# Forming five quads of weight sums from the staged plain quads in the last phase, with a written split plan per step

## The chip, the cores and the metric

The kernel runs on one core of one Trainium2 chip. The metric is the device time of one launch in microseconds (us); lower is better. The times shown are medians over runs. A profile is of one execution, and it lists its own time beside its span (first to last instruction).

## The reference, cut to what matters

A parallel block on `x` of shape (2048, 640), all in float32:

```python
xn = _layernorm(x, axis=-1)
return x + _A_ref(xn, A_wqkv, A_wo) + _B_ref(xn, B_w_gate, B_w_up, B_w_down)

# A: sliding-window attention, 32 heads of 20, window 256, then  o @ wo      (640 x 640)
# B: h = gelu(xn @ w_gate) * (xn @ w_up);  h @ w_down                        (1728 x 640)
```

The attention output `o` (640 features) and the first 1664 features of `h` are put one below the other, and `w_down` and `wo` too. So the last product is one product with 18 row blocks of 128, plus a rest of 64 features of `h`.

## The kernel before

Products are made in float32 from pairs of reduced-precision numbers. Every operand is **split** into a high part (ScalarE copies it into the type fp32r) and a low part (VectorE subtracts the high part from the original), and three matmuls (high by high, low by high, high by low) stand for one.

There are three phases. In the first, layer norm, projections and attention run, with a part of the gate and up products as filler. In the **gate phase** (about 652 to 838 us of the profile) the remaining gate and up products are made by `gate_up_pair`. In the **last phase** (from 837.8 us) the output product runs. Both phases after attention use a seven-product scheme for 2 x 2 blocks (Strassen's, in Winograd's form), which needs sums of blocks of both operands beside the plain blocks.

**Steps of the last phase.** The output is made in `NP` = 8 parts `p` of 256 rows. A part has ten steps: nine quads `k` = 0 to 8 (a quad is a 2 x 2 arrangement of four weight blocks of 128 x 320: two row blocks by two column halves), and one short step "e" for the rest of 64 features. Steps are numbered `n` = 0 to 79; "e" is the fifth of each ten (n = 4, 14, 24). Part 0 and the first four quads of part 1 are **plain** (24 matmuls per step, no sums needed). From n = 15 on (part 1, k = 4 to 8, and all later parts) a step takes 21 matmuls and needs, beside the plain quad `("b", k)`, the quad of sums `("t", k)`. From part 2 on the order of k is 4 to 8 and then 0 to 3.

**One pass of the step loop** (lines 1344 to 1372) puts into the queues: `load_step(n + 4)` on SP (activations of a later step), `split_step(n + 2)` (L1071: high part on ScalarE L1084, low part on VectorE L977), then `prepare(n)` (splits of weight quads for later), then the matmuls of step n (`terms`, L1142). At the last step of a part comes `drain`, which adds the PSUM banks of the finished part to the output rows on VectorE (L1165) and stores them from SP (L1168). The matmuls of the next part write the same banks, so the first of them waits for the first additions of the drain. The order on PE, ScalarE (ACT), VectorE (DVE) and SP is as written; each engine works off its queue in that order.

**Weight quads.** A quad is loaded into a staging tile `stg` (three buffers, L954) by `fetch`, and split by `high_quad` (ACT, L970) and `low_quad` (DVE, L974, which shows as its helper's line L977). In the last phase the fetches go out from ACT's own queue (`eng=nc.scalar`), so a fetch waits there for its staging buffer to come free, and what follows on ACT waits behind it. Quads b0 to b3 are split at the end of the gate phase; b4 to b8 and all t quads in the last phase. Two t quads have no room of their own: t7 is written over block 1 of b4 to b7, and t3 over block 1 of b0 to b3 (`borrow`), once the plain steps no longer need them.

**Where the sums are made before.** In the gate phase, `Job("t", q)` loads the plain quad into a tile `ats`, forms the four sums in place with four VectorE instructions (L977, L993, L977, L977), and stores the tile to `wtd[q]` in DRAM. Nine such jobs run among the others (`Job("o")` divides the attention output by its softmax sums, `Job("r")` makes the reciprocals). `work(cap)` is called between the products of `gate_up_pair` and does at most `cap` items. In the last phase all nine t quads are fetched from `wtd`.

**The plan before.** `tasks` gives one quad per step: the high part of b4 to b8 at n = 1 to 5, of t4, t5, t6, t7, t8, t0, t1, t2 at n = 6 to 13, and of t3 at n = 15. The low part follows one step later. The fetch of a quad goes out three places ahead, from ACT's queue, in n = 2 to 12.

Of the kernel before, what the change touches and what calls it, by code (L numbers as in the profile page):

```python
# [9 lines left out]
F32 = mybir.dt.float32  # L10
F32R = mybir.dt.float32r
BF = mybir.dt.bfloat16
AF = mybir.ActivationFunctionType
OP = mybir.AluOpType
# [20 lines left out]
HD = D // 2  # L35
HR = 5
NQD = 9
# [24 lines left out]
def block_kernel(ctx, tc, x, wqk, wv, wgu, wdo, wdl, out):  # L62
    nc = tc.nc

    const = ctx.enter_context(tc.tile_pool(name="const", bufs=1))
    dram = ctx.enter_context(tc.tile_pool(name="dram", bufs=1, space=DRAM))
# [16 lines left out]
    od = [dram.tile([D, C], F32, name=f"od{c}") for c in range(NC)]  # L83
    sd = [dram.tile([H, C], F32, name=f"sd{c}") for c in range(NC)]
    td = [{i: dram.tile([128, 2, C], F32, name=f"td{p}{i}") for i in (1, 2, 3, 4)} for p in range(NC // 2)]
    wtd = [dram.tile([128, 4, HD], F32, name=f"wtd{q}") for q in range(NQD)]
    rd = [dram.tile([H, C], F32, name=f"rd{c}") for c in range(NC)]
    hd = [dram.tile([NC, 128 if f < NF - 1 else 64, C], F32, name=f"hd{f}") for f in range(NF)]

# [836 lines left out]
    quads, staged, raws, ats = {}, {}, {}, {}  # L926
    place = {("b", 0): "xh1", ("b", 1): "xl1", ("b", 2): "xh0", ("b", 3): "xl0",
             ("t", 0): "xh2", ("t", 1): "xl2", ("t", 2): "xh3", ("t", 8): "xl3"}
    borrow = {7: 4, 3: 0}
# [10 lines left out]
    def four(t):  # L940
        return t.rearrange("p k (h n) -> p (k h) n", h=2)

    def fetch(kind, q, where="stg", eng=nc.sync):
        if where == "wr":
            ts = [wrp.tile([128, KT, 128], F32, name="wr", tag="wr").rearrange("p k m -> p (k m)") for _ in range(2)]
        elif where != "stg" and where != "at":
            ts = [tp.tile([128, D], F32, name=f"b{n}{q}", tag=f"x{n}{where}") for n in "hl"]
        if where != "stg" and where != "at":
            for i, t in enumerate(ts):
                nc.sync.dma_start(t, wdo[q][:, i])  # L950
            staged[kind, q] = [(t.rearrange("p (h n) -> p h n", h=2), slice(2 * i, 2 * i + 2)) for i, t in enumerate(ts)]
            return
        pool, bufs = (rp3, 3) if where == "stg" else (cp, 3)
        t = pool.tile([128, 4, HD], F32, name="stg", tag=where, bufs=bufs)  # L954
        eng.dma_start(t, four(wdo[q]) if kind == "b" else wtd[q])
        if kind == "t" and q in borrow:
            staged[kind, q] = [(t[:, i:i + 1], slice(i, i + 1)) for i in range(4)]
        else:
            staged[kind, q] = [(t, slice(0, 4))]

    def parts(kind, q):
        for raw, dst in staged[kind, q]:
            if kind == "t" and q in borrow:
                yield raw, quads["b", borrow[q] + dst.start], slice(1, 2)
            else:
                yield raw, slots(kind, q)[0][0], dst

    def high_quad(kind, q):
        for raw, t, dst in parts(kind, q):
            nc.scalar.activation(t[:, 0, dst], raw, AF.Copy)  # L970

    def low_quad(kind, q):
        for raw, t, dst in parts(kind, q):
            sub(t[:, 1, dst], raw, t[:, 0, dst].bitcast(F32))  # L974

    def sub(o, i, j, op=OP.subtract):
        nc.vector.tensor_tensor(out=o, in0=i, in1=j, op=op)  # L977

    class Job:
# [3 lines left out]
        def load(self):  # L983
            kind, i = self.kind, self.i
            if kind == "r":
                t = self.t = c2.tile([128, 128], F32, name="rc", tag="rc", bufs=2)
                nc.sync.dma_start(t, sd[i].rearrange("h (a t) -> (h a) t", a=4))
                self.items = [lambda: nc.vector.reciprocal(t, t)]
            elif kind == "t":
                t = self.t = cp.tile([128, 4, HD], F32, name="ats", tag="at", bufs=3)  # L990
                nc.sync.dma_start(t, four(wdo[i]))
                self.items = [lambda: sub(t[:, 0], t[:, 1], t[:, 0]), lambda: sub(t[:, 1], t[:, 3], t[:, 1], OP.add),
                              lambda: nc.vector.scalar_tensor_tensor(t[:, 3], t[:, 3], -1.0, t[:, 0],  # L993
                                                                     op0=OP.mult, op1=OP.subtract),
                              lambda: sub(t[:, 2], t[:, 2], t[:, 3], OP.add)]
            else:
                n = len(self.ks)
                if self.ks[0] == 0:
                    rbs[i] = c2.tile([128, C], F32, name="rb", tag="rb")
                    for k in range(4):  # L1000
                        nc.sync.dma_start(rbs[i][32 * k:32 * k + 32], rd[i])
                rows = self.rows = od[i][self.ks[0] * 128:(self.ks[-1] + 1) * 128].rearrange("(k p) t -> p k t", p=128)
                t = self.t = cp.tile([128, n, C], F32, name="ato", tag="at", bufs=3)
                nc.sync.dma_start(t, rows)
                self.items = [lambda k=k: sub(t[:, k], t[:, k], rbs[i], OP.mult) for k in range(n)]
# [8 lines left out]

    rbs = {}
    jobs = [Job("r", 0), Job("r", 1)]
    for c, qs_, r in ((0, (4, 5), 2), (1, (6, 7), 3), (2, (8, 0), None), (3, (1, 2), None)):
        jobs += [Job("t", q) for q in qs_] + [Job("o", c, (0, 1, 2)), Job("o", c, (3, 4))]
        jobs += [Job("r", r)] if r else []
    jobs.append(Job("t", 3))  # L1020
    going = []
    hook = [0]

# [219 lines left out]
    def split_later_xs(i, nxt=None):  # L1243
        def fn():
            split_xs(1, i, later[i])
            if nxt:
                later[nxt] = load_xs(1, nxt)
        return fn
# [9 lines left out]
    for j, f in enumerate(range(NFA, NF - 1)):  # L1258
        end = f + 1 == NF - 1
        first, second = {i: [] for i in range(4)}, {i: [] for i in range(4)}  # L1260
        first[0] += carry
        if j == 0:
            first[0].append(split_later_xs(2, 4))
            first[2].append(split_later_xs(1))
            first[3].append(split_later_xs(3))
            second[0].append(split_later_xs(4))
        if not end:
            nxt_w, sums = [], {}

            def next_tiles(j=j, raws=raws_next[f + 1]):  # L1270
                nxt_w.append(w_tiles(raws, *pools[(len(sets) + j + 1) % 2]))

            first[3].append(next_tiles)
            items = w_sums(raws_next[f + 1], sums)
            second[2] += items[0:2]
            second[3].append(items[2])
            carry = list(items[3:5])
            if f + 2 < NF - 1:
                second[3].append(load_next(f + 2))
        if j:  # L1280
            for i, n in enumerate((0, 3, 1, 2)):
                first[i].append(work(n))
        if not end:
            for i, n in enumerate((2, 3, 1, 1) if j else (0, 2, 1, 1)):
                second[i].append(work(n))
        else:
            fetch("b", 0, "wr")
            raw13 = cp.tile([128, D], F32, name="raw13", tag="r13")
            nc.sync.dma_start(raw13, wdl)
        gate_up_pair(f, w, 0, first)  # L1290
        if end:
            assert not jobs and not going
            for n in range(2):
                load_step(n)
            fetch("b", 1, "at")

            def quad(q):
                high_quad("b", q)
                low_quad("b", q)

            second[0].append(lambda: quad(0))
            second[0].append(lambda: [fetch("b", 2, "02"), fetch("b", 3, "03")])
            second[1].append(lambda: [split_step(0), load_step(2)])
            second[2].append(lambda: [split_step(1), quad(1), load_step(3)])
            second[3].append(lambda: [quad(2), split_step(2)])
        stores = gate_up_pair(f, w, 1, second, end)
        if end:
            quad(3)
        if not end:
            w = nxt_w[0], sums  # L1310
# [9 lines left out]
    psn = p3.enter_context(tc.tile_pool(name="psn", bufs=1, space=PSUM, reuse_waits="tile"))  # L1320
    w13 = rp3.tile([128, 2, D], F32R, name="w13")

    order_ = [("b", q) for q in range(4, NQD)] + [("t", q) for q in (4, 5, 6, 7, 8, 0, 1, 2)]
    tasks = {n + 1: q for n, q in enumerate(order_)}
    tasks[len(order_) + 2] = "t", 3
    turns = list(tasks)
    fetch_at = {0: [tasks[n] for n in turns[1:3]]}
    for i, n in enumerate(turns[3:]):
        fetch_at.setdefault(turns[i] + 1, []).append(tasks[n])

    def prepare(n):
        if n in tasks:
            high_quad(*tasks[n])
        if n - 1 in tasks:
            low_quad(*tasks[n - 1])
        if n == 2:
            nc.scalar.activation(w13[:, 0], raw13, AF.Copy)
            sub(w13[:, 1], raw13, w13[:, 0].bitcast(F32))
        for q in fetch_at.get(n, ()):
            fetch(*q, eng=nc.scalar if n else nc.sync)  # L1340

    fetch("b", 4)
    held = []
    for n, (p, k) in enumerate(steps):
        i = n % (NQD + 1)
# [71 lines left out]
```

## Time and profile before

| quantity | value |
|---|---|
| device time, median of 3 runs | 1090.1 us (1087.86 to 1091.1) |
| device time of the profiled execution | 1088.03 us |
| its span | 1086.3 us |
| busy: PE, DVE, ACT, POOL | 1068.9, 766.0, 511.9, 340.7 us |
| granted TensorE clock | 1.00 |
| DMA traffic | 162.31 MB, mean 149 GB/s |
| `ats<-wdo`, `wtd<-ats`, `stg<-wtd` transfers | 9 each, 640 KB |
| gate phase, matmuls L884 on the chain that ended last | 666.34 to 825.7 us, 702 matmuls |
| last phase, first and last matmul L1142 | 837.79 us, about 1083 us |

The chain that ended last, by engine: PE 84%, DVE 8%, DMA 4%. A matmul row with a count ("x96") is a run of instructions merged into one; its start and length are those of the run. A bracket at the end of a row gives the idle time of that engine just before it and what ended it. The ends of matmuls are modelled: a 128x320 matmul is listed with about 0.31 us, while in a run they start 0.147 us apart.

### The profile page before, as it was taken

To read this page: it belongs to the slowest core of one execution; us is meant where nothing else is said; L and a number is where in the kernel's file an instruction comes from. 1 tells how busy PE (TensorE), PEld (TensorE's weight loads), DVE (VectorE), ACT (ScalarE), POOL (GpSimd) and SP (SyncE) were. 2 spreads that over 40 slices of the span, in tenths; PEclk is the share of its full clock that TensorE was granted. 3 is DMA by queue.
4 is the path that set the end of the run, shared out by engine and by line. 5 is a ranking of instruction groups with operands and counts; after the bars stand their busy time and mean duration, and the time that the engine had idled before them with its cause. 6 is when DMAs were issued, how large, how long until landed. Compare 5 with 4: busy or idle time off the path is not lost.

```text
span 1086.3 us, 20868 instructions
## 1 busy us (share of the span) xinstructions
PE 1068.9 (98%) x7253; PEld 856.2 (79%) x7253; DVE 766.0 (71%) x2030; ACT 511.9 (47%) x1037; POOL 340.7 (31%) x513
## 2 busy tenths in 40 slices
PE   8999999999999999999999999999999989999998
PEld 7887767666778766676766668888888988999998
DVE  7755667666666576666767636888875669888887
ACT  4434655565644555465545465322234544333332
POOL 5022755577653373645446250211110000000000
PEclk9999999999999999999999999999999999999999
DMA  5651453546442244434233215588856873343433
GB/s 205 198 151 50 119 153 98 154 116 183 138 141 82 71 141 127 131 94 126 87 117 109 80 59 195 185 271 291 266 203 235 303 244 113 118 131 120 132 125 115
DMA packets 96058, 162.31 MB, mean 149 GB/s; under 512 B 13248, under 2 KB 57920, under 8 KB 95952
## 3 DMA queue, kind: packets, MB, share of 16 engines
q1 hardware_dynamic: 93280, 153.50, 44.6%
q10 hardware_dynamic: 2672, 7.47, 2.1%
q8 instruction: 57, 0.93, 0.4%
q14 instruction: 49, 0.40, 0.1%
HBM read 104.40 MB, written 56.23 MB: 148 GB/s over the span
## 4 chain that ended last, share of the span: by engine, by line
PE 84%; DVE 8%; DMA 4%; issue 1%; ACT 1%; SPq 0%; POOL 0%; ACTq 0%; DVEq 0%
PE ps_d L101 25%; PE ps L1142 15%; PE ps_g L884 15%; PE ps_o L547 8%; PE ps_e L520 7%; PE ps_m L464 7%; PE ps_v L101 5%; DVE junk L466 2%; PE ps_g L101 1%; DMA stg<-wtd 1%; DMA stg<-wdo 1%; DMA xi<-x 1%; PE ps_t L177 1%; DMA out<-xr 1%; DVE xi L160 1%
## 5 line engine op out<-in xcount | busy, mean ns | idle before, releaser
L466 DVE CUSTOM_DVE_ANT_0 junk<-ps_m,mask 128x384 bf16<-128x384 f32 (+2 forms) x512 | 271.9, 531 | 177.8 <-PE ps_m L464 132.9
L522 ACT ACTIVATE P<-ps_e 128x512 f32<-128x512 f32 (+2 forms) x384 | 197.6, 568 | 59.7 <-PE ps_e L520 52.9
L1142 PE MATMUL ps<-wb,at 128*128 128x320 f32 x999 | 157.8, 310 | 4.8 <-ACT wb L970 2.2
L1142 PEld LDWEIGHTS ps<-wb,at 128*128 128x128 f32 x999 | 149.0, 188 | 6.9 <-ACT wb L970 2.4
L533 POOL TENSOR_SCALAR_AFFINE_SELECT P<-P 128x512 f32<-128x512 f32 x128 | 86.6, 676 | 159.1 <-ACT P L522 155.0
L101 PE MATMUL ps_d<-xh,wql 128*128 128x512 f32 x430 | 129.2, 410 | 0.0
L101 PE MATMUL ps_d<-xh,wqh 128*128 128x512 f32 x430 | 128.5, 409 | 0.1
L101 PE MATMUL ps_d<-xl,wqh 128*128 128x512 f32 x430 | 128.6, 408 | 0.0
L464 PE MATMUL ps_m<-ks,qs 120*128 120x128 bf16 (+1 forms) x704 | 120.1, 275 | 1.4 <-DVE mx L466 1.1
L520 PE MATMUL ps_e<-qs,ks 122*128 122x128 bf16 (+2 forms) x704 | 112.4, 277 | 0.2
L520 PEld LDWEIGHTS <-ks 122*128 122x128 bf16 x704 | 49.9, 98 | 52.9 <-issue 41.9
L101 PEld LDWEIGHTS ps_d<-xl,wqh 128*128 128x128 f32 x430 | 78.3, 188 | 15.3 <-issue 1.2
L1142 PE MATMUL ps<-wt,at 128*128 128x320 f32 x552 | 89.0, 309 | 0.8 <-DVE xr L1165 0.8
L101 PEld LDWEIGHTS ps_d<-xh,wqh 128*128 128x128 f32 x430 | 77.7, 188 | 15.0 <-issue 1.0
L101 PEld LDWEIGHTS ps_d<-xh,wql 128*128 128x128 f32 x430 | 77.9, 189 | 14.6 <-issue 1.0
L464 PEld LDWEIGHTS <-qs 120*128 120x128 bf16 x704 | 62.2, 98 | 29.2 <-issue 11.6
L547 PE MATMUL ps_o<-P,v 128*32 128x384 f32 (+2 forms) x1408 | 84.3, 386 | 0.0
L1142 PEld LDWEIGHTS ps<-wt,at 128*128 128x128 f32 x552 | 82.9, 188 | 1.2 <-DVE xr L1165 1.0
L536 POOL TENSOR_SCALAR_AFFINE_SELECT P<-P 128x512 f32<-128x512 f32 x112 | 73.7, 668 | 27.9 <-ACT P L522 27.8
L238 POOL TENSOR_TENSOR pt<-r,pt 128x512 bf16<-128x512 f32 x40 | 46.8, 1171 | 103.7 <-ACT pt L237 89.6
L1096 ACT ACTIVATE at<-ss 128x512 fp32r<-128x512 f32 x59 | 37.3, 631 | 79.9 <-DVE ss L977 79.8
L547 PEld LDWEIGHTS ps_o<-P,v 128*32 128x32 f32 x1408 | 40.1, 110 | 39.5 <-issue 28.6
(185 smaller groups left out, 1701.3 us busy)
## 6 DMA issues: line engine op xcount, KB each, us to landing
hr<-hd SPq DMA_DIRECT2D x104, 128.0 KB
hd<-he SPq DMA_DIRECT2D x50, 256.0 KB
wr<-wgu SPq DMA_DIRECT2D x27, 320.0 KB
qs<-qd SPq DMA_DIRECT2D x32, 240.0 KB
ks<-kd SPq DMA_DIRECT2D x32, 240.0 KB
ats<-wdo SPq DMA_DIRECT2D x9, 640.0 KB
wtd<-ats SPq DMA_DIRECT2D x9, 640.0 KB
stg<-wtd ACTq DMA_DIRECT2D x9, 640.0 KB
```

Source lines behind the costliest of these rows:

```text
L101: nc.tensor.matmul(ps, a(k), b(k), start=n == 0, stop=n == 3 * nk - 1)
L238: nc.gpsimd.tensor_tensor(out=pt[:, l, :], in0=r, in1=pt[:, 1, :], op=OP.subtract)
L464: nc.tensor.matmul(ps[:, lo:hi], lh, rhs, start=True, stop=True)
L466: nc.vector.tensor_tensor_reduce(out=junk[:, 0:n], in0=ps[:, 0:n], in1=mask[:, 384 - n:384], scale=1.0, scalar=NEG, op0=OP.add, op1=OP.max ...
L520: nc.tensor.matmul(ps[:, col:col + n], k[0:QROWS, j, kc:kc + 128], q[0:QROWS, j, q0:q0 + n], start=True, stop=True)
L522: nc.scalar.activation(pt[:, j, lo:hi], ps[:, lo:hi], AF.Exp, scale=SCALE)
L533: nc.gpsimd.affine_select(out=a, in_=a, pattern=[[0, 4], [1, 128]], compare_op=OP.is_ge, fill=0.0, base=0, channel_multiplier=-1)
L536: nc.gpsimd.affine_select(out=a, in_=a, pattern=[[0, 4], [-1, 128]], compare_op=OP.is_ge, fill=0.0, base=-1, channel_multiplier=1)
L547: nc.tensor.matmul(o[32 * j:32 * j + 32, q0:q0 + n], v[:, w0_:w0_ + 32], pt[:, j, col:col + n], start=i == 0, stop=i == len(todo) - 1, ski ...
L884: nc.tensor.matmul(ps, i, j, start=first and n == 0, stop=n == len(work) - 1, skip_group_check=True)
L1096: nc.scalar.activation(hi[:, 3:7], s, AF.Copy)
L1142: nc.tensor.matmul(ps[bank][:, 0:HD], *work[bank][j], start=bank not in begun, stop=final[p, bank] == n and j == len(work[bank]) - 1, skip ...
```

## The change

Jobs "t" remain for q = 0 to 3 only; the gate phase makes and stores four quads of sums, and not nine. The caps of `work` become smaller. For q = 4 to 8 the last phase forms the sums in the staging tile of the plain quad, in place, right after that quad has been split (`sum_quad`), and then splits the same tile again as the t quad. Those five fetches from `wtd` fall away. The even rhythm of one quad per step gives way to a written plan, in which "f" is a fetch on ACT's queue, "h" a high part, "l" a low part, "s" the four sums, "p3i" one of the four parts of t3 (high, then low):

```diff
-    wtd = [dram.tile([128, 4, HD], F32, name=f"wtd{q}") for q in range(NQD)]
+    wtd = [dram.tile([128, 4, HD], F32, name=f"wtd{q}") for q in range(4)]
...
+    def sum_items(t):
+        return [lambda: sub(t[:, 0], t[:, 1], t[:, 0]), lambda: sub(t[:, 1], t[:, 3], t[:, 1], OP.add),
+                lambda: nc.vector.scalar_tensor_tensor(t[:, 3], t[:, 3], -1.0, t[:, 0],
+                                                       op0=OP.mult, op1=OP.subtract),
+                lambda: sub(t[:, 2], t[:, 2], t[:, 3], OP.add)]
+
+    def sum_quad(q):
+        (t, _), = staged["b", q]
+        for fn in sum_items(t):
+            fn()
+        staged["t", q] = [(t[:, i:i + 1], slice(i, i + 1)) for i in range(4)] if q in borrow else [(t, slice(0, 4))]
...
-    for c, qs_, r in ((0, (4, 5), 2), (1, (6, 7), 3), (2, (8, 0), None), (3, (1, 2), None)):
+    for c, qs_, r in ((0, (0, 1), 2), (1, (2,), 3), (2, (3,), None), (3, (), None)):
...
-    jobs.append(Job("t", 3))
...
-            for i, n in enumerate((0, 3, 1, 2)):
+            for i, n in enumerate((0, 2, 1, 1)):
                 first[i].append(work(n))
         if not end:
-            for i, n in enumerate((2, 3, 1, 1) if j else (0, 2, 1, 1)):
+            for i, n in enumerate((1, 2, 1, 1) if j else (0, 2, 1, 1)):
                 second[i].append(work(n))
...
-    order_ = [("b", q) for q in range(4, NQD)] + [("t", q) for q in (4, 5, 6, 7, 8, 0, 1, 2)]
-    tasks = {n + 1: q for n, q in enumerate(order_)}
-    tasks[len(order_) + 2] = "t", 3
-    turns = list(tasks)
-    fetch_at = {0: [tasks[n] for n in turns[1:3]]}
-    for i, n in enumerate(turns[3:]):
-        fetch_at.setdefault(turns[i] + 1, []).append(tasks[n])
+    plan = {1: "hb4 lb4 s4", 2: "hb5 ht4 lb5 lt4", 3: "fb7 hb6 lb6 s5", 4: "ht5 lt5 s6", 5: "fb8 hb7 ht6 lb7 lt6",
+            6: "ft0 hb8 lb8 s8", 7: "ht8 lt8 s7", 8: "ft1 ht0 lt0", 9: "ft2 ht7", 10: "lt7 ht1 lt1",
+            11: "ft3 ht2 lt2", 13: "p30 p31 p32", 15: "p33"}
 
     def prepare(n):
-        if n in tasks:
-            high_quad(*tasks[n])
-        if n - 1 in tasks:
-            low_quad(*tasks[n - 1])
+        for op in plan.get(n, "").split():
+            kind, q = op[1], int(op[-1])
+            if op[0] == "f":
+                fetch(kind, q, eng=nc.scalar)
+            elif op[0] == "s":
+                sum_quad(q)
+            elif op[0] == "p":
+                for raw, t, dst in list(parts("t", 3))[q:q + 1]:
+                    nc.scalar.activation(t[:, 0, dst], raw, AF.Copy)
+                    sub(t[:, 1, dst], raw, t[:, 0, dst].bitcast(F32))
+            else:
+                (high_quad if op[0] == "h" else low_quad)(kind, q)
         if n == 2:
             nc.scalar.activation(w13[:, 0], raw13, AF.Copy)
             sub(w13[:, 1], raw13, w13[:, 0].bitcast(F32))
-        for q in fetch_at.get(n, ()):
-            fetch(*q, eng=nc.scalar if n else nc.sync)
+        if n == 0:
+            fetch("b", 5)
+            fetch("b", 6)
```

The matmuls, their order and their operands stay as they were.

More of the change, by code (lines that the diff above doesn't have):

```diff
@@ L991, in load @@
                 nc.sync.dma_start(t, four(wdo[i]))
[L992 to L995, printed above, removed]
+                self.items = sum_items(t)
             else:
```

## The prediction

> **What bounds the kernel now.** I read in this order: the windows table (which engine is full in which phase), the waits of PE, then the timelines of PE, DVE and ACT where PE waits. A gate-phase row of the windows table, then the waits of PE in the last phase, longest first:
>
> ```profile
> 720.00:760.00 40.00, 40.00 (x178) 33.13 (x177) 33.40 (x56) 11.59 (x22) 5.99 (x4) 1.00 0.88 296
> ```
> ```profile
> PE ps L1142 <- ACT wb L970: 2.2, 1, 2.2
> PE ps L1142 <- ACT at L1088: 0.8, 1, 0.8
> PE ps L1142 <- DVE xr L977: 0.8, 1, 0.8
> PE ps L1142 <- DVE xr L1165: 0.8, 1, 0.8
> PE ps L1142 <- DVE at L977: 0.7, 3, 0.3
> PE ps L1142 <- ACT m L1153: 0.2, 1, 0.2
> ```
>
> In the gate phase PE is busy 40.00 of 40.00 us, and the list of its waits from 640 to 838 us is empty. What the change takes away there is not on the path. In the last phase PE waits 5.5 us, all of it between 870 and 916 us:
>
> ```profile
> 853.04 17.76 PE L1142 MATMUL ps<-wb,at 128*128 128x320 f32 x120
> 873.00 14.31 PE L1142 MATMUL ps<-wb,at 128*128 128x320 f32 x96 [2.20 <-ACT wb L970]
> ...
> 892.38 0.41 PE L1142 MATMUL ps<-wb,at 128*128 128x320 f32 x1 [0.81 <-ACT at L1088]
> ...
> 907.91 0.71 PE L1142 MATMUL ps<-wb,at 128*128 128x320 f32 x3 [0.80 <-DVE xr L977]
> 909.38 2.22 PE L1142 MATMUL ps<-wt,at 128*128 128x320 f32 x12 [0.76 <-DVE xr L1165]
> ```
>
> From 915.6 us on PE doesn't wait until the final drain. So the time is won or lost between 838 and 916 us. There the pace is set by the DVE queue. Its rows at the turn of part 0, then the four sums of one quad in the gate phase, then the ACT queue:
>
> ```profile
> 870.97 1.48 DVE L977 TENSOR_TENSOR wt<-stg,wt 128x1280 fp32r<-128x1280 f32 x1
> 872.37 1.68 DVE L1165 TENSOR_TENSOR xr<-ps,xr 128x320 f32<-128x320 f32 x4
> ```
> ```profile
> 731.67 1.00 DVE L977 TENSOR_TENSOR ats<-ats 128x320 f32<-128x320 f32 x2
> 732.71 0.49 DVE L993 SCALAR_TENSOR_TENSOR ats<-ats 128x320 f32<-128x320 f32 x1
> 733.23 0.49 DVE L977 TENSOR_TENSOR ats<-ats 128x320 f32<-128x320 f32 x1
> ```
> ```profile
> 858.57 1.27 ACT L970 ACTIVATE wb<-stg 128x1280 fp32r<-128x1280 f32 x1 [1.27 <-DMA stg<-wdo]
> 859.50 0.33 ACTq L955 DMA_DIRECT2D stg<-wtd  x1
> 859.93 0.63 ACT L1084 ACTIVATE at<-hr 128x512 fp32r<-128x512 f32 x1
> 861.97 1.28 ACT L970 ACTIVATE wt<-stg 128x1280 fp32r<-128x1280 f32 x1 [1.40 <-DMA stg<-wtd]
> ```
>
> The wait before 873.00 is put down to ACT, but a drain add starts at 872.37 and one add takes 0.48, so it ends at 872.85: PE waits for the first add of the drain, which stands on DVE behind a low part of 1.40 (870.97 to 872.37). The fetch at 859.50 goes out 0.07 after the low part that frees its buffer, and 5.2 to 5.7 us pass until its quad is split.
>
> **Gate phase: nothing.** Removed are 20 DVE sums of 0.48 (9.7 us) and ten transfers of 640 KB from SP's queue. PE's cover is its own work: DVE has 6.6 of 40 us free already. Without that cover it would still be no wait of PE. Matmuls of 512 columns start 0.227 apart over the 702 of the chain and 0.2265 in quiet stretches, so less DMA traffic is worth at most 702 x 0.0005, about 0.3 us. I take 0.
>
> **Last phase to the turn of part 0: a loss.** Added are 5 x 4 sums on DVE, and t4, t5, t6 and t8 are split here beside b4 to b8 as before, but s8, s7 and t0 too come ahead of the drain. I go through the DVE queue from the row of the low part of step 3 (844.64). Start-to-start costs from rows: low part of an activation 0.61, of a quad 1.41, of step "e" 0.46, of w13 0.75; the sums of a quad 2.05 (731.67 to 733.72), 1.97 until the next may start. DVE stands idle where ACT is held: a high part takes 1.27 on ACT, and it can start only when the sums are done (0.07 later), and a fetch on ACT (0.44) waits for the low part that frees its buffer.
>
> - n=1: 0.61 + 1.41 + 1.97, to 848.63. n=2: 0.46 + 1.41 + 1.41 + 0.75, to 852.66.
> - n=3: 0.61, idle 0.53 (fetch of b7 behind the low part of t4, then the high part of b6), 1.41 + 1.97, to 857.18.
> - n=4: 0.61, idle 0.85 (high part of t5 behind its sums), 1.41 + 1.97, to 862.02. n=5: 0.61 + 1.41 + 1.41, to 865.45.
> - n=6: 0.61, idle 1.29 (fetch of t0, then the high part of b8), 1.41 + 1.97, to 870.73.
> - n=7: 0.61, idle 0.85 (t8), 1.41 + 1.97, to 875.57. n=8: 0.61 + 1.41, to 877.59. n=9: 0.61, to 878.20.
>
> The first drain add ends at 878.69, and step 10 starts at **878.75** instead of 873.00: a loss of **5.75**. (30.0 us of work and 3.5 idle; the same queue needs about 17 us of work before.) The loss shows in pieces, since PE also waits for activations whose low part stands behind sums: steps run 24 x 0.1467 = 3.52, so "e" waits about 0.8 (for w13), n=6 0.5, n=7 1.2, n=9 1.6, n=10 3.7. Queued behind the ACT fetches are high parts of quads; b8 lands about 865.8 (860.2 + 5.6) and is wanted at 866.0, the tightest of the loads; the others have over 0.9 us to spare, t3 aside.
>
> **From there to step 22: a gain.** Steps 10 to 21 hold 96 + 8 + 7 x 21 = 251 matmuls, 36.8 us at 0.1467. Before they take 42.45 (873.00 to 915.45, the start of step 22 with its own wait of 0.49 counted): 5.6 us of waits, of which the profile lists 3.3, since modelled ends hide the rest. They come from low parts of t8, t0, t1, t2 and t3 (five of 1.4 to 1.7) on DVE at 882 to 901, where a seven-product step already takes 2.5 us of DVE out of 3.1, and from an ACT stall of 4.7 (fetch of t1 until an output store had landed). In the plan only t7, t1 and t2 stand behind the drain, done by 887.1; then DVE has the activations and four parts of 0.42. Counted on, the split for step 15 ends at 890.0 and PE wants it at 894.0; at step 16 the margin is 4 (or 1, with the stall of the rival below). So the 5.6 come back. Bounds: none (0) and all (5.6); I take all, since the later turns, with the same drain and no quads, show no wait.
>
> **Sum:** +5.75 - 5.6 = +0.1 us on the span of 1086.3. The profiled execution took 1088.03, 1.7 more than its span; the median is 2.1 above that. So 1090.1 + 0.1, and I lean 0.3 to the slow side for the tight load of b8: **1090.5**.
>
> A rule of the Trainium skill bears on the 2.05: VectorE: DVE Perf Modes, section "The DRAIN you can't avoid", says the pipeline empties behind every operation and a semaphore between chained operations costs nothing extra. Here the trace differs: four drain adds start 0.40 apart (1.68 for four), sums that feed one another 0.52. By the rule a quad of sums would take 1.6, five of them 1.85 less, and the time would be 1088.7.
>
> **Rivals.** (1) Slower: t3's fetch (n=11) is the one ACT fetch behind the stores of the drain. In the trace before, the fetch of t1 stood 4.7 us until a store issued at 873.32 had landed (6.83). Stores of the new drain go out to about 880.6, so the fetch would stand until 887.4, t3 lands at 893, and ACT is blocked at its first part while the splits of steps 16 on stand behind it. PE wants step 16 at 897.1; that path takes 3 us more, so it decides from a landing after 894, and then costs 1 us per us until the 5.6 are gone: +3.5 to +5.7, **1093.6 to 1095.8**. For: that the stall exists. Against: it just fits by the measured landings.
> (2) Faster: a shorter DVE chain. With the sums 0.40 apart 1.85 less, and with the idle 3.5 filled too 5.4 less: **1088.7**, at the utmost **1085.1**. For: independent adds do run 0.40 apart. Against: the rows of these very sums.
> (3) The gate phase gains after all by lighter DMA and DVE: 0.3, or beyond it what no row shows; against: no wait of PE. **1089.5** to 1086.
> (4) The hand-overs between ACT and DVE add up worse, or b8 is late: each us late at n=6 moves the turn by one: +2 to +4, **1092 to 1094**.
>
> **Chances.** Forecast 0.55, (1) 0.20, (2) 0.14, (3) 0.03, (4) 0.08. About 0.3% (3.3 us) is what a measurement of this kernel can tell from no change. Beyond 3.3 us on the fast side lie most of (2)'s lower half, some of (3): 0.13 with a share of the forecast's spread. On the slow side (1), half of (4) and some of the spread: 0.29. Within: 0.58. The range, 1086.6 to 1095.0, leaves out the outer part of (1) and of (2); the forecast's own is 1088.5 to 1092.5.
>
> **What would show it.** Right: DVE from 844 to 878 without a gap over 1.5 us; new waits of PE at n=4, 6, 7 and 9 and a longer one at the turn (step 10 near 878.7); none from step 15 to 22; step 22 near 915.6; the gate phase as before. Wrong: a turn before 876, sums 0.40 apart, or waits of PE left between 892 and 917.

## The result and the profile after

The changed kernel takes **1093.85 us** (median of 9 executions, 1091.98 to 1096.7), the kernel before 1086.38 (median of 9, 1084.98 to 1091.1): a ratio of **1.0063, 95% interval 1.0045 to 1.0081**, some 7 us slower. The prediction was 1090.5 with a range of 1086.6 to 1095.0. The time lies in the range, but the difference does not lie where the forecast had it: the median of 1090.1 that the forecast started from stood high, and instead of +0.1 the change costs about 7.

First the waits of PE from 640 us to the end in the kernel after (sum of us, number of waits, longest):

```profile
PE ps L1151 <- DVE xr L1174: 3.7, 1, 3.7
PE ps L1151 <- DVE at L989: 2.6, 3, 1.4
PE ps_g L884 <- ACT gs L898: 1.0, 1, 1.0
PE ps L1151 <- DVE w L989: 0.9, 1, 0.9
PE ps_g L884 <- DVE qp L887: 0.6, 1, 0.6
```

Two things stand here that were not there before: the waits on the drain and on activations have grown to 7.2 us, and the gate phase (ps_g, line 884), where PE had no wait in the profile of before, has two. Then PE's timeline in the last phase of the kernel after:

```profile
842.84 14.24 PE L1151 MATMUL ps<-wb,at 128*128 128x320 f32 x96
...
858.14 1.29 PE L1151 MATMUL ps<-w,he 128*128 128x320 f32 x7 [0.92 <-DVE w L989]
863.26 3.79 PE L1151 MATMUL ps<-wb,at 128*128 128x320 f32 x24 [0.17 <-DVE at L989]
868.07 7.30 PE L1151 MATMUL ps<-wb,at 128*128 128x320 f32 x48 [1.03 <-DVE at L989]
876.80 3.64 PE L1151 MATMUL ps<-wb,at 128*128 128x320 f32 x23 [1.42 <-DVE at L989]
884.10 15.61 PE L1151 MATMUL ps<-wb,at 128*128 128x320 f32 x96 [3.67 <-DVE xr L1174]
899.55 1.34 PE L1151 MATMUL ps<-w,he 128*128 128x320 f32 x8
```

The five waits are the chain of the sums on DVE, piece by piece as they were worked out. From the step at 884.10 on there is no bracket any more: the waits behind the turn are gone. But the 96 matmuls behind the turn take 15.61 us. In the kernel before the same 96 take 14.31 (its row at 873.00). The windows table says why; the column that counts is the last but two, the granted clock:

```profile
835.00:880.00 45.00, 41.46 (x259) 39.00 (x258) 37.98 (x52) 23.76 (x30) 0.00 (x0) 1.00 0.68 235
880.00:900.00 20.00, 16.33 (x103) 16.10 (x103) 16.37 (x31) 10.13 (x19) 0.00 (x0) 0.91 0.74 236
900.00:930.00 30.00, 30.00 (x207) 29.96 (x206) 25.29 (x59) 10.62 (x22) 0.00 (x0) 1.00 0.39 124
```

Behind the wait of 3.67 us the clock is 0.91 over 20 us, and 1.00 again afterwards.

The gate phase's new waits start on SP's queue. Its issues around 780 us in the kernel after, and then the DVE rows of the division jobs:

```profile
773.63 0.32 SPq L1020 DMA_DIRECT2D wtd<-ats  x1
785.60 1.71 SPq L1010 DMA_DIRECT2D rb<-rd  x4
787.41 0.38 SPq L1013 DMA_DIRECT2D ato<-od  x1
```
```profile
783.70 1.88 DVE L989 TENSOR_TENSOR ato<-ato,rb 128x512 f32<-128x512 f32 x3
...
793.12 0.69 DVE L989 TENSOR_TENSOR ato<-ato,rb 128x512 f32<-128x512 f32 x1 [3.00 <-DMA ato<-od]
```

The row tile rb has one buffer. The load of the next chunk's rb stands on SP until DVE has done the last divisions of the chunk before (783.70 + 1.88 = 785.58; the load goes out at 785.60, after a wait of 11.6 us). The fetch of ato queues behind it, lands late, and DVE stands 3.00 us for it, with the gate products that PE waits for behind. Before, two sum jobs lay between any two chunks and gave the load its time; now the divisions of the last chunk follow those of the third directly.

To see the terms apart, here are the landmarks of two pairs of profiled executions: the pair of the first result, and a second pair (c0, g0 below). The start of the run is beyond the change: in the first 20 us, where both kernels run the same code, the clock was 0.83 in the profile of after and 1.00 in those of before, c0 and g0.

| us | before | after | difference | c0 | g0 | difference |
|---|---|---|---|---|---|---|
| first matmul of the gate phase (line 884) | 666.17 | 669.10 | +2.93 | 667.37 | 667.43 | +0.06 |
| from there to the first of the last phase | 171.62 | 173.74 | +2.12 | 171.38 | 173.94 | +2.56 |
| from there to step 10 | 35.21 | 41.26 | +6.05 | 35.45 | 41.20 | +5.75 |
| from step 10 to the last group of matmuls | 208.00 | 203.67 | -4.33 | 205.88 | 204.86 | -1.02 |
| span | 1086.3 | 1093.1 | +6.8 | 1085.4 | 1092.8 | +7.4 |

### The profile page after: what moved, and what is told of

It reads as the page before. It is cut to its first block, busy times and chain, and to the rows that moved or that the text cites. A ratio compares the mean times of both kernels' runs of the same rounds, so it can differ in the third digit from the quotient of the medians.

```text
span 1093.1 us, 20844 instructions
## 1 busy us (share of the span) xinstructions
PE 1073.3 (98%) x7253; PEld 861.1 (79%) x7253; DVE 767.4 (70%) x2030; ACT 512.2 (47%) x1037; POOL 340.5 (31%) x513
## 4 chain that ended last, share of the span: by engine, by line
PE 86%; DVE 9%; DMA 2%; issue 2%; ACT 1%; SPq 0%; POOL 0%; DVEq 0%; ACTq 0%
PE ps_d L101 24%; PE ps L1151 19%; PE ps_g L884 13%; PE ps_o L547 8%; PE ps_e L520 7%; PE ps_m L464 7%; PE ps_v L101 5%; DVE junk L466 2%; PE ps_g L101 1%; DVE wb L989 1%; PE ps_t L177 1%; DVE wt L989 1%; DMA xi<-x 1%; PE ps_d L338 1%; DVE stg L989 1%
```

## The experiments

All were timed in five rounds, each beside the kernel before on the same chip. The chips differ from run to run, so it is the ratios that can be compared.

**c0, the kernel before once more**, no edit.

> The kernel before, once more, for its trace on this chip and its spread. Theory and rivals alike: ratio 1.000 within 0.0015; no wait of PE in the gate phase; step 10 begins 35.2 us after the first matmul of the last phase; if slow clock at the start comes by chance and not by the change, some executions of this kernel show it too (3 us each).

1087.82 us, ratio 0.9995 (0.9984 to 1.0007). It is here for its profile. PE's timeline at the turn of part 0 and at that of part 1:

```profile
874.20 14.31 PE L1142 MATMUL ps<-wb,at 128*128 128x320 f32 x96 [2.43 <-DVE xr L1165]
...
905.49 0.71 PE L1142 MATMUL ps<-wb,at 128*128 128x320 f32 x3 [0.24 <-ACT m L1153]
907.00 0.71 PE L1142 MATMUL ps<-wb,at 128*128 128x320 f32 x3 [0.80 <-DVE xr L977]
908.46 2.22 PE L1142 MATMUL ps<-wt,at 128*128 128x320 f32 x12 [0.76 <-DVE xr L1165]
```

The waits at 892 to 896 of the profile that the prediction was made from (0.81, 0.18, 0.16) are not there, and not in e2 either, which has the same last phase. ACT stands behind the output store here too, but for 3.72 us and not for 4.69:

```profile
879.67 0.63 ACT L1084 ACTIVATE at<-hr 128x512 fp32r<-128x512 f32 x1 [3.72 <-DMA out<-xr]
```

This high part starts 5.47 behind step 10 (879.67 - 874.20), where in the first profile it starts 7.71 behind it (880.71 - 873.00). That these 2.2 us make the difference is likely and not shown. Steps 10 to 21 take 40.33 here (874.20 to 914.53, the start of step 22 with its wait), 3.5 above the 36.8 of the matmuls alone, and not 5.6.

**g0, the kernel after once more**, no edit, beside g1.

> The changed kernel once more, on the same chip as the next two. Theory: ratio 1.0055 to 1.0063; waits of PE in the gate phase of 1.0 and 0.6 us, the turn about 41.3 us after the first matmul of the last phase, a lower clock behind it.

1093.09 us, ratio 1.0045 (1.003 to 1.006). The turn's wait is 3.68 again, and the 96 matmuls behind it take 16.81.

**e1, the gate phase of before with the last phase of after.** The nine sum jobs and the larger caps are back, and all sums are stored.

```diff
-    for c, qs_, r in ((0, (0, 1), 2), (1, (2,), 3), (2, (3,), None), (3, (), None)):
+    for c, qs_, r in ((0, (4, 5), 2), (1, (6, 7), 3), (2, (8, 0), None), (3, (1, 2), None)):
...
+    jobs.append(Job("t", 3))
```

> The gate phase of before (nine jobs of sums, old caps), the last phase of after; the stored sums of quads 4 to 8 are not read. Theory (the change costs 2.1 in the gate phase by a new wait and about 1.8 in the last phase: the turn 6.0 later, 1.3 by a lower clock behind that wait, 5.6 given back): about +1.8 us, ratio 1.0017, no wait of PE in the gate phase, step 10 near 41.3 us after the first matmul of the last phase. Rival A (all of the measured 6.8 lies in the last phase): ratio 1.006. Rival B (the loss lies in the gate phase): ratio 1.000.

1092.12 us, ratio 1.0037 (1.0023 to 1.0052): with the gate phase of before the change still costs about 4 us, twice what I expected. The waits of the last phase are those of after (1.01, 0.17, 1.04, 1.42, 3.66), and the 96 matmuls behind the turn take 16.87, 2.56 more than the 14.31 at full clock. Not as expected, PE waits once in the gate phase as well (1.17 us at 787.88), after DVE stood 2.00 us for the load of a sum job. The phase takes 172.88 here (668.23 to 841.11), 1.3 and 1.5 more than in before and c0, in an execution of 1094.3 us, the slowest of the six. So the last phase need not cost all of the 4 us.

**e2, the gate phase of after with the last phase of before.** Only four quads of sums are made, and t4 to t8 are fetched from `wdo`, so the sums of quads 4 to 8 are left out of the computation.

```diff
-        eng.dma_start(t, four(wdo[q]) if kind == "b" else wtd[q])
+        eng.dma_start(t, four(wdo[q]) if kind == "b" or q > 3 else wtd[q])
```

> The gate phase of after, the last phase of before; the quads t4 to t8 are read from the plain weights, so their sums are left out of the computation. Theory: +2.1 us, ratio 1.002, PE waits 1.0 and 0.6 for ACT and DVE behind a DVE item that waits for its load, last phase as before (step 10 at 35.2). Rival A: ratio 1.000 and no such wait. Rival B: ratio 1.005 or more.

1090.04 us, ratio 1.0016 (1.0003 to 1.0029): the gate phase alone costs, too. The two waits of ps_g are back (1.1 and 0.7 us), and the gate phase takes 173.93 (667.45 to 841.38). Its last phase is not quite that of before, as PE's row at the turn shows:

```profile
877.39 15.86 PE L1141 MATMUL ps<-wb,at 128*128 128x320 f32 x96 [3.01 <-DVE xr L1164]
```

The wait is 3.01 instead of 2.20 and 2.43, and the 96 matmuls take 1.55 more. The excesses of e1 and e2 add up to 0.0053, which lies between the two ratios of the whole change (1.0045 and 1.0063).

**e3, the kernel after with one sum job ahead of each chunk's divisions**, so that no two chunks follow each other directly.

```diff
-    for c, qs_, r in ((0, (0, 1), 2), (1, (2,), 3), (2, (3,), None), (3, (), None)):
+    for c, qs_, r in ((0, (0,), 2), (1, (1,), 3), (2, (2,), None), (3, (3,), None)):
```

> After, with one job of sums ahead of the divisions of each of the four chunks, where after has two, one, one and none. Theory (with no job between two chunks, the load of the next reciprocals into the single buffer waits for the last division of the chunk before it, and the next division waits for its load): both waits of PE in the gate phase go, 2.1 us less than after, ratio 1.0044 instead of 1.0063. Rival (the wait comes from the smaller caps, or from DMA traffic): the waits stay, ratio 1.006.

1092.4 us, ratio 1.0034 (1.0022 to 1.0046). PE has no wait in the gate phase any more, which takes 171.50 (669.03 to 840.53); the last phase is as in after (turn 3.68, 96 matmuls in 15.84).

**g1, the kernel after with two buffers for rb**, to test the cause itself.

```diff
-                    rbs[i] = c2.tile([128, C], F32, name="rb", tag="rb")
+                    rbs[i] = c2.tile([128, C], F32, name="rb", tag="rb", bufs=2)
```

> The changed kernel with two buffers for the reciprocals rb and nothing else. Theory (the next reciprocals' load stands in SP's queue until the last division of the chunk before, and holds the load of the rows behind it): that wait of SP goes, the row load goes out earlier, both waits of PE in the gate phase go, 1.7 to 2.1 us less than the run above. Rival (the row load is held by its own buffer or by the lookahead of three hooks, not by rb): the waits stay and so does the time.

1091.77 us, ratio 1.0027 (1.0015 to 1.0039), against 1.0045 for g0 on the same chip; the intervals overlap. The trace decides. SP's issues and the same DVE row in g1:

```profile
772.43 2.33 SPq L1010 DMA_DIRECT2D rb<-rd  x4
775.16 0.38 SPq L1013 DMA_DIRECT2D ato<-od  x1
```
```profile
788.46 0.68 DVE L989 TENSOR_TENSOR ato<-ato,rb 128x512 f32<-128x512 f32 x1
```

The load of rb goes out at 772.43 instead of 785.60, the division has no bracket, and PE is busy 195.00 of 195.00 us from 640 to 835 (193.42 in after). The gate phase takes 171.55 us (667.53 to 839.08) instead of g0's 173.94. That the single buffer made the waits of the gate phase is shown.

**f1, e3 with 22 idle matmuls behind step 9**, into a bank that nothing reads any more, so that PE works through most of the wait at the turn.

```diff
+        if n == NQD:
+            for _ in range(22):
+                nc.tensor.matmul(ps[7][:, 0:HD], quads["b", 8][:, 0, 0, 0:128], quads["b", 8][:, 0, 1],
+                                 start=True, stop=True, skip_group_check=True)
```

> As e3, with 22 matmuls into an unused bank put behind step 9, so that PE is busy for about 3.2 of the 3.7 us that it waits at the turn of part 0; their results are not read. Theory (a wait of over 3 us lowers the granted clock for some us behind it, 1.3 to 2.6 us of loss): the 96 matmuls behind the turn take 14.3 instead of 15.6 to 16.9, the clock from 875 to 925 us is 1.00, ratio about 1.0015 to 1.002. Rival (the lower clock comes by chance and has nothing to do with the wait): they stay at 15.6 or more, ratio 1.0034 or above.

1090.09 us, ratio 1.0009 (0.9997 to 1.0021), against 1.0034 for e3. PE's timeline at the turn in f1:

```profile
875.45 3.39 PE L1383 MATMUL ps<-wb 128*128 128x320 f32 x22
879.28 14.31 PE L1151 MATMUL ps<-wb,at 128*128 128x320 f32 x96 [0.44 <-DVE xr L1174]
```

Step 10 starts 41.23 behind the first matmul of the phase (838.05), hardly earlier than in e3 (41.49), so DVE is about as late as before. Only the clock is kept, and the 96 matmuls take 14.31. Work that computes nothing makes the kernel some 2.5 us faster: that the lower clock comes from the long wait is shown. Its size differs from one execution to the next; in e3's profile it is 1.53 (15.84 - 14.31).

**f3, e3 without the 20 sum instructions.**

```diff
         (t, _), = staged["b", q]
-        for fn in sum_items(t):
-            fn()
```

> As e3, but the 20 sum instructions are left out (t4 to t8 are split from the plain quads, so the sums of quads 4 to 8 are left out of the computation); the plan is the same. Theory (the sums themselves, 5 x 2.0 us of DVE, make the turn late): wait at the turn about 2, no lower clock, ratio about 0.997. Rival (the plan's order and its hand-overs between ACT and DVE make the turn late, not the sums): wait at the turn 3 or more, ratio 1.0025 or more.

1081.83 us, ratio 0.9933 (0.9914 to 0.9952), better than expected: with 10 us less on DVE the turn has no wait at all, where I had expected 2. The rest of the change (five sum jobs and five fetches less, and the order of the splits) is worth 7 us by itself; the sums cost 10.6 against e3.

**f2, e3 with s7 and the splits of t8 and t0 put behind the turn**; t1 to t3 are split later still.

```diff
-    plan = {1: "hb4 lb4 s4", 2: "hb5 ht4 lb5 lt4", 3: "fb7 hb6 lb6 s5", 4: "ht5 lt5 s6", 5: "fb8 hb7 ht6 lb7 lt6",
-            6: "ft0 hb8 lb8 s8", 7: "ht8 lt8 s7", 8: "ft1 ht0 lt0", 9: "ft2 ht7", 10: "lt7 ht1 lt1",
-            11: "ft3 ht2 lt2", 13: "p30 p31 p32", 15: "p33"}
+    plan = {1: "hb4 lb4 s4", 2: "hb5 ht4 lb5 lt4", 3: "fb7 hb6 lb6 s5", 4: "ht5 lt5", 5: "fb8 hb7 s6 lb7",
+            6: "ht6 lt6 hb8 lb8", 7: "ft0", 8: "s8", 9: "ht8", 10: "lt8 s7", 11: "ht7 ft1 lt7", 12: "ht0 lt0 ft2",
+            13: "ft3 ht1 lt1", 17: "ht2 lt2", 21: "p30 p31 p32 p33"}
```

> As e3, all sums in place on DVE as in after, but in another plan: the sums of quads 7 and 8 and the splits of t7, t8 and t0 stand behind the drain of part 0, t1 to t3 still later. Theory (the loss is DVE work that stands ahead of the drain, and behind it there is room): the wait at the turn is under 1 us, the clock stays 1.00, the waits of steps 4 to 9 are about 2, none over 1 behind the turn; by the ledger 5.4 less waiting than after, and 1.5 more of clock: ratio about 0.997. Rival (the sums are too much for DVE wherever they stand): waits of 4 us or more come back between steps 15 and 22, ratio 1.002 or more.

1084.58 us, ratio **0.9964 (0.9949 to 0.9979)**: faster than both kernels. PE's timeline in f2:

```profile
854.84 1.30 PE L1151 MATMUL ps<-w,he 128*128 128x320 f32 x7 [0.45 <-DVE w L989]
859.96 28.29 PE L1151 MATMUL ps<-wb,at 128*128 128x320 f32 x191 [0.16 <-DVE at L989]
```

191 matmuls run through the turn as one row. All 20 sums are still made, 16 of them ahead of the turn. The drain on DVE starts at 873.24, 33.24 behind the first matmul of the phase (840.00), where after has 40.63. Of these 7.4 us 4.8 are the low parts and sums that were moved (1.41 + 1.41 + 1.97), and 1.85 are gaps: DVE's bracketed ones ahead of the drain are 0.45, 0.74, 1.12 and 0.73 in after, and 0.45 and 0.74 in f2. The other 0.75 stays open. The expectation counts the sums of quad 8 among those behind the drain; in the plan they stand at step 8, ahead of it.

**f4, the kernel before with the drain ahead of the splits of step 9 and the low parts of all t quads on GpSimd.**

```diff
-            sub(t[:, 1, dst], raw, t[:, 0, dst].bitcast(F32))
+            if kind == "t":
+                nc.gpsimd.tensor_tensor(out=t[:, 1, dst], in0=raw, in1=t[:, 0, dst].bitcast(F32), op=OP.subtract)
+            else:
+                sub(t[:, 1, dst], raw, t[:, 0, dst].bitcast(F32))
...
-        prepare(n)
+        if n != NQD:
+            prepare(n)
...
+        if n == NQD:
+            prepare(n)
```

> The kernel before with two edits in its last phase: at step 9 the drain stands ahead of the splits, and the low parts of all t quads are made by GpSimd. No sums in the last phase. Theory (all waits of the last phase before come from quad splits on DVE ahead of the drain and behind it): wait at the turn of part 0 about 0.9, none at the turn of part 1, 4 to 5 us less than before: ratio about 0.9955. Rival (GpSimd takes twice as long for a low part and holds the staging buffers, or slows DVE): ratio 1.000 or more.

1090.18 us, ratio 1.0013 (1.0000 to 1.0026): the gain that I expected (0.9955) did not come. DVE and then GpSimd (POOL) in f4, same time:

```profile
864.76 3.05 DVE L980 TENSOR_TENSOR at<-hr,at 128x512 fp32r<-128x512 f32 x1 [1.59 <-ACT at L1087]
868.38 2.81 DVE L980 TENSOR_TENSOR at<-hr,at 128x512 fp32r<-128x512 f32 x1 [0.57 <-ACT at L1087]
871.71 2.78 DVE L980 TENSOR_TENSOR at<-hr,at 128x512 fp32r<-128x512 f32 x1 [0.52 <-ACT at L1087]
```
```profile
864.28 9.66 POOL L975 TENSOR_TENSOR wt<-stg,wt 128x1280 fp32r<-128x1280 f32 x3 [59.79 <-ACT wt L970]
```

The same subtraction takes DVE 0.69 when GpSimd rests (861.07). Work taken off DVE came back as DVE instructions that take four times as long; the turn's wait is 3.54, and with it the 96 matmuls behind take 15.85.

**g2, e1's gate phase, no sums in the last phase, all quads fetched, with a plan of my own.**

```diff
+    plan = {1: "hb4", 2: "hb5 lb4 fb7", 3: "hb6 lb5 fb8", 4: "hb7 lb6 ft4", 5: "hb8 lb7 ft5", 6: "ht4 lb8 ft6",
+            7: "ht5 lt4 ft7", 8: "ht6 lt5 ft8", 10: "lt6 ht7", 11: "ht8 lt7 ft0", 12: "lt8 ht0", 13: "lt0 ft1",
+            17: "ht1 lt1 ft2", 21: "ht2 lt2 ft3", 25: "p30 p31 p32 p33"}
```

> The kernel before (nine jobs of sums in the gate phase, nine fetches, no sums in the last phase), but with a written plan: nothing of quads ahead of the drain of step 9, t0 to t3 split at steps 12 to 26. Theory (what made f2 faster than before is the order of the splits, not where the sums are made): waits of the last phase about 1.4 us by the ledger instead of 6, ratio 0.9945 to 0.997. Rival (f2 gained by the sums in place, with fewer transfers): ratio 0.999 to 1.001, with the waits of before at the turns.

1090.32 us, ratio 1.0015 (1.0002 to 1.0027): missed. DVE has 10 us less to do than in f2, and still PE waits 2.50 at the turn. PE at the turn, then DVE and ACT in g2:

```profile
875.71 14.31 PE L1151 MATMUL ps<-wb,at 128*128 128x320 f32 x96 [2.50 <-DVE xr L1174]
```
```profile
861.43 0.69 DVE L989 TENSOR_TENSOR at<-hr,at 128x512 fp32r<-128x512 f32 x1 [1.20 <-ACT at L1093]
862.04 1.48 DVE L989 TENSOR_TENSOR wb<-stg,wb 128x1280 fp32r<-128x1280 f32 x1
864.70 0.69 DVE L989 TENSOR_TENSOR at<-hr,at 128x512 fp32r<-128x512 f32 x1 [1.18 <-ACT at L1093]
```
```profile
863.60 0.33 ACTq L955 DMA_DIRECT2D stg<-wtd  x1
864.04 0.63 ACT L1093 ACTIVATE at<-hr 128x512 fp32r<-128x512 f32 x1 [0.69 <-DVE wb L989]
```

From 861 us to the drain DVE stands idle 1.1 to 1.2 us in every step, and a step is 3.27 long (861.43 to 864.70). The low part at 862.04 ends at 863.5, the fetch into its buffer goes out at 863.60, the activations' high part starts behind that fetch at 864.04, and DVE's low part of it at 864.70: a ring of hand-overs through two in-order queues.

**h1, g2 with each fetch one place later on ACT.** The high parts of b7 to t0 move one place later as well, and t1 to t3 are split by step 21. DVE has the same low parts ahead of the drain.

```diff
+    plan = {1: "hb4", 2: "hb5 lb4", 3: "hb6 fb7 lb5", 4: "fb8 lb6", 5: "hb7 ft4 lb7", 6: "hb8 ft5 lb8",
+            7: "ht4 ft6 lt4", 8: "ht5 ft7 lt5", 10: "ht6 ft8 lt6", 11: "ht7 ft0 lt7", 12: "ht8 ft1 lt8",
+            13: "ht0 ft2 lt0", 14: "ht1 ft3 lt1", 17: "ht2 lt2", 21: "p30 p31 p32 p33"}
```

> g2_plan_without_sums again (no sums in the last phase, the gate phase of the kernel before, 9 quads of plain and 9 of summed weights fetched), with every fetch one place later in ScalarE's queue: behind the high part of the step after, not behind the low part of its own step, and with t0 to t3 split by step 21 instead of 25. The amount of work is the same. Theory: in g2 each step was a ring of hand-overs: ScalarE's fetch waits for VectorE's low part that frees the buffer, the activations' high part stands behind that fetch, VectorE's low part of the activations behind that high part, and the low part of the next quad behind it. VectorE's rows there were 3.28 apart per step (861.43, 864.70, 867.99, 871.25) with only 2.1 of work in each, so the drain add came 2.5 late, with or without sums. One place later the fetch finds its buffer free: VectorE needs 2.1 per step, the wait of TensorE at the turn of part 0 falls from 2.50 to under 0.5, step 10 starts 33.0 to 33.5 behind the first matmul of the last phase (35.51 in g2), the waits at the turn of part 2 (0.73 and 0.75) go too, the clock stays at 1.00, and the time is some 4 us below g2's, a ratio of 0.996 to 0.998 to the kernel before. Rival: the drain add is late because of the number of instructions ahead of it or of landings of the quads, not of the ring: the wait at the turn stays at 2 to 3 and the ratio at 1.000 to 1.002.

1083.81 us, ratio **0.9956 (0.9943 to 0.9970)**, a little below the 0.996 to 0.998 expected; by the ratios it is some 6 us below g2, where 4 were expected. PE's row through the turn, PE's waits and the drain on DVE in h1:

```profile
856.12 31.84 PE L1151 MATMUL ps<-wb,at 128*128 128x320 f32 x216
```
```profile
PE ps L1151 <- DVE xr L1174: 0.5, 1, 0.5
PE ps L1151 <- DVE at L989: 0.3, 1, 0.3
PE ps_g L884 <- DVE qp L887: 0.2, 1, 0.2
```
```profile
871.68 0.98 DVE L1174 TENSOR_TENSOR xr<-ps,xr 128x320 f32<-128x320 f32 x2
873.04 0.49 DVE L1174 TENSOR_TENSOR xr<-ps,xr 128x320 f32<-128x320 f32 x1 [0.39 <-PE ps L1151]
```

PE runs through the turn of part 0 without a wait; the wait of 0.5 is at 905.96, at the turn of part 1. The drain starts 30.81 us behind the first matmul of the phase (840.87), in g2 34.88 (875.08 - 840.20), and DVE now waits for PE. So the order on ACT's queue made g2's drain late.

How much of that is the ring is not separated. At DVE's low part of the activations of step 6, h1 stands 13.90 behind the first matmul of the phase (854.77 - 840.87) and g2 17.94 (858.14 - 840.20): the lead of 4 us is there before the five steps of 3.27. In g2 the fetch of b8 ahead of it goes out at 857.01, 1.56 after the low part that frees its buffer (853.97 + 1.48); what holds it is open. The ring then keeps DVE from making up the delay.

h1 makes all its sums in the gate phase as the kernel before does, with the same transfers, and is as fast as f2 (the intervals overlap). So f2 and h1 gain by the order of splits and fetches; that sums made in place gain anything by themselves is not shown. A version with h1's order, fewer fetches and two buffers of rb was not tried.

## Why the prediction was right or wrong

**"Last phase to the turn of part 0: a loss" of 5.75: right.** Step 10 came 6.05 and 5.75 us later in the two pairs. The pieces stood at 0.8, 0.5, 1.2, 1.6 and 3.7, and were 0.92, 0.17, 1.03, 1.42 and 3.67. The drain add started 40.63 us behind the first matmul of the phase; counted was 40.41.

**"From there to step 22: a gain" of 5.6: the mechanism was right, the size was not.** The waits did vanish. But 5.6 was read from one execution. In c0, where ACT stood behind the output store for 3.72 us instead of 4.69, there are 3.5 to give back. This is the first mis-sized term: 2.1 us.

**What the sum lacked: the clock behind the long wait.** I had forecast the wait of 3.7 and counted it as 3.7. The clock behind it costs 1.3 (after), 1.5 (e3), 2.6 (e1) and 2.8 us (g1) more. With it the row from step 10 on closes: 5.6 given back less 1.3 is 4.3 in the first pair, 3.5 less 2.5 is 1.0 in the second. f1 shows it as a cause.

**"Gate phase: nothing": wrong.** I looked at what the jobs that go away cost, and not at what they kept apart. Without them rb's single buffer ties the last two chunks together, and the phase grows by 2.12 and 2.56 us. Of this the waits list 1.6 in after and 1.8 in g0, since modelled ends hide the rest: the matmul at 796.23 in after is due 0.227 behind the one at 794.82, and comes 1.18 later than that. In e3 and g1 the waits are gone and the phase has its old length.

**The sum, +0.1:** by the second pair 0.06 + 2.56 + 5.75 - 3.5 + 2.5 = 7.37 us, against a difference of 7.4 in the spans. That the time lies in the range all the same is luck: the median of 1090.1 that the sum started from stood 3.7 above the 1086.38 of the comparison, and the range reached up to 1095.0 for rival (1), which did not come. For a change of more than 3.3 us to the slow side the prediction had a chance of 0.29.

**The rivals.** (1) ACT blocked by t3's fetch: not seen, the fetch went out at 889.82 and PE doesn't wait behind the turn. (2) Sums 0.40 apart: not seen. The rows in after (lines 989 and 978) start at 851.90, 852.95 and 853.48 for the first pair and the two others, 0.52 apart, and the next work at 854.00. The Trainium skill, VectorE: DVE Perf Modes, section "The DRAIN you can't avoid", has a semaphore between chained operations cost nothing extra, by a measurement on eight copies; the rows here differ, 0.52 against the 0.40 of independent adds, and they decide. (3) A gain in the gate phase: the reverse came. (4) b8 late: not seen, DVE's gap there was 1.12, and 1.29 was counted.

## What to carry to other kernels

When work moves onto an in-order engine ahead of a hand-over, its place in the queue counts beside its busy time: putting 4.8 us of splits and sums behind the turn, in an order with fewer gaps, made the changed kernel faster than the one before, and a fetch that waits for a buffer holds up everything queued behind it on its engine. Price a new wait of PE of 3 us or more with what the clock loses behind it, and read the gain that a change can give back from more than one execution. Look at a removed step also for what it kept apart, single buffers above all.

## What the runs showed of the hardware

**The clock behind a wait.** The 96 matmuls behind the turn took 14.31 us after waits of 0.44 (f1), 2.20 (before), 2.43 (c0) and 2.50 (g2), and 15.86 after 3.01 (e2), 15.85 after 3.54 (f4), 15.61 to 17.10 after 3.66 to 3.68 (after, e1, e3, g0, g1). So in these profiles, one or two of each kernel, the step lies between 2.5 and 3.0 us of listed wait, and the price varies by 1.5 us for one and the same wait. The Trainium skill, TensorE: Matmul & The Clock Gate, section "Part 1: The HAM clock gate (the "warmup" mystery)", has a free-running window of about 3.4 us, whose phase varies from run to run, and half the clock after an idle one. The runs agree in kind, and with the spread of the price; 3.01 of listed wait was already enough here. In g2 two waits of 0.73 and 0.75 close together cost clock too (12 matmuls in 3.39 us instead of 1.92, a clock of 0.74 from 940 to 945 us). A like pair in c0, 0.80 and 0.76, cost hardly any (2.22).

**DVE beside GpSimd.** A DVE subtraction of two inputs of 128x512 takes 0.69 us, and 2.78 to 3.05 while GpSimd runs a subtraction of 128x1280, which takes some 3 us itself (DVE's takes 1.48). The Trainium skill, GPSIMD Engine Reference, section "1. Specifications", has the two engines share their SBUF interfaces, with contention for DVE instructions with two SBUF inputs. The runs agree: the four drain adds at 874.42 in f4, with one input in PSUM, take 1.67 beside GpSimd, as they do without it in before (1.68). Not every subtraction is slowed; one at 876.01, beside GpSimd's parts of 128x320, took 0.68. The lengths of the slow ones look as if DVE waited for the end of GpSimd's instruction, which no run here separates from sharing.

**The start of a run.** Over the first 20 us the clock was 0.83 in the profiles of after, e3, g2 and h1, 0.91 in those of e1, e2, f2 and f3, and 1.00 in those of before, c0, f1, f4, g0 and g1, with the same code in all of them; after and g0 are the same kernel. The start of the gate phase moves with it: 666.17 to 667.53 us at 1.00, 667.45 to 668.60 at 0.91, 668.39 to 669.10 at 0.83. h1, with its 0.83 and a start at 668.95, is among the fastest. So the start follows no edit; what sets it is open.
